# A residual block of a diffusion model on Trainium2: the second normalization's scales handed out one group sooner, with the written order and the engines of the scaled copies planned anew

## The chip, the cores and the metric

The kernel runs on one core of a Trainium2 chip. A core has five engines that work side by side, each through its own list of instructions: PE (TensorE, matrix products; its weight loads are shown apart as PEld), DVE (VectorE), ACT (ScalarE), POOL (GpSimd) and SP (SyncE, which here only starts DMA transfers; POOL starts some too). The metric is the device time of one execution in microseconds (us), lower is better. The profile comes from one execution that was recorded by the hardware profiler.

## The reference

The block takes `x` of shape (2, 512, 64, 64), a time embedding `t_emb` of (2, 1152), two pairs of group norm parameters and three weight tensors, and returns the same shape as `x`. There are 4 groups of 128 channels, so one group of the normalization is exactly one tile of 128 partitions.

```python
def gn(z, gamma, beta):
    zr = z.reshape(B, G, (C // G) * H * W)          # G = 4
    mu = zr.mean(-1).reshape(B, G, 1)
    var = ((zr - mu) ** 2).mean(-1).reshape(B, G, 1)
    zn = ((zr - mu) / jnp.sqrt(var + 1e-5)).reshape(B, C, H, W)
    return zn * gamma.reshape(1, C, 1, 1) + beta.reshape(1, C, 1, 1)

h = conv3(_silu(gn(x, g1, be1)), w1)                # conv3: 3x3, zero padding
h = h + (_silu(t_emb) @ w_emb).reshape(B, C, 1, 1)
h = conv3(_silu(gn(h, g2, be2)), w2)
return x + h
```

## The kernel before, in words

*Layers, chunks, groups.* There are two layers, one for each convolution. A layer is worked off in four chunks (two images, each in two halves of 32 rows), and a chunk in four groups, one for each tile of 128 output channels. So a layer has 16 groups and the kernel 32; "group (1,2)" is group 2 of layer 1. A group keeps PE busy for about 13 us.

*The convolution.* It is not done as nine products but in transformed form: the activations of a chunk are transformed to `V`, the weights to `U`, PE multiplies them, and the products are transformed back. Some products use the untransformed weights `R`.

- `produce_V` makes `V` of one chunk. For each of the four channel tiles, SP loads a piece of the layer's input into `ak` (L621; in layer 1 from the scratch tensor `h_scr` that layer 0 wrote), ACT applies the normalization and SiLU in one instruction (L628, with the scales `sc_all` and biases `nb_all`), and DVE transforms: copies of `ak` by a factor, and L642, L649, L669, L679, L559, L564.
- `prep_U` makes `U` of one output tile and half of the input channels: SP loads `R` and `g1t` (L402), four scaled copies write `U` and `g1t` in place, a POOL DMA that accumulates (L433) and DVE additions (L422) follow, and `nest_U` (L395).
- The matmuls of a group are at L935 (128x512, into the PSUM tiles `acc` and `mid`), at L943 (128x256, into `nst`) and L1038. Evacuations are scaled copies from PSUM: `rm<-nst`, `rm<-mid`, `ring<-acc`. DVE transforms back in L988 to L1009 and others; a POOL DMA adds one part (L1070).
- In layer 0 the result goes to `h_scr` by SP (L1074), and two ACT instructions (L796) for each group take its sum and sum of squares. In layer 1 POOL transfers add `x` (L803) and store the output (L809).

*The second normalization.* When both halves of an image have gone through layer 0, `gn2_me` (L508 to L519, DVE) makes means from the sums of L796 and the embedding. `gn2_scale` (L521 to L527) calls `gn_scale_bias` (L316 to L342): a small PE matmul (L319) sums over partitions and spreads the result, DVE copies and combines (L321, L330, L331, L332), POOL raises the variance to the power -1/2 (L339), DVE multiplies and adds (L340 to L342, L526, L527) and so fills `sc_all` and `nb_all` of layer 1. L628 of that image in layer 1 reads them.

*What sets the order.* The program is written out group by group; a small scheduler (`_Background`) deals out the steps of `produce_V` and `prep_U` to the groups by due times. The function `aux_plan` says at which group `gn2_scale` is emitted: for image 0 in group 11 of layer 0, for image 1 in group 3 of layer 1. But the order in which the engines execute is not that one. After emission, `in_order` takes for each of the five engines a list of numbers, `ORDER` (L64 to L173), and pins the engine's instructions to that order: number k is the k-th instruction that was emitted for this engine. DMA starts on POOL and SP are in these lists as well. When an instruction waits, everything behind it on its engine waits too.

*Which engine copies.* A scaled copy is one instruction with a source, a target and a factor. `scaled_copy` (L302 to L309) can make it on ACT (L308) or DVE (L309), and the string `FLIP` has one bit for each of its 406 calls, in the order of emission: evacuations (`evac`) go to ACT unless their bit is 1, all others (`times`) go to DVE unless it is 1. In the profile, the engine and the tiles tell what such a row is: L308 ACT `rm<-nst` is an evacuation of the nested products, L309 DVE `U<-R` a weight copy.

Of the kernel before, what the change touches and what calls it, by code (L numbers as in the profile page):

```python
# [18 lines left out]
class _Background:  # L19
# [45 lines left out]
0-31 90-122 32-43 123 44-56 124 156 125 157-162 126 163-172 127-136 173-181 137-153 182-187 154-155 57-73 188 74-79  # L65
189-252 80-89 254 286 255 287-317 256-258 253 320-335 259-277 336-351 278-285 318 358 370-385 359-360 352-353
386-401 354-355 319 356-357 364-369 408-410 420-423 402-403 424-435 361-362 414 404-407 415-419 363 411-413 458 461
436-451 459 452-453 460 462-463 454 464-465 455 466 470-485 467 456-457 468-469 486-501 511-512 508 502-503 509
514-519 504-507 510 513 520-525 544-549 526-533 550 534-536 551 537 552-553 538-542 592-593 543 554-559 568 560-565
580 566-567 569-570 581-583 571-572 594 573-575 595 576 584-585 596-600 586-589 601-608 624-625 590-591 626-634 609  # L70
635-638 577-579 639-644 610-621 645 648 622-623 646-647 649-654 673 661 674 655-659 675 660 662-670 689 705-716 671
717-721 672 722-725 676 726-728 677-678 690-701 737 702-703 738 704 679-680 749-750 681-687 751-752 688 753-760
739-744 729-730 745 761 731-736 762 746 763 777 747-748 778-779 793-815 780-786 825-826 787-789 816 827 790-792 837
828 764-776 829-835 838 836 839-848 817 849 865 850-851 818 852 819-822 866-867 853-857 823 868-869 824 870-871 858
872 859 873 860-864 874-879 881 880 882-903 905-907 904 913 908 914-915 925 909 916 926 910-912 937-938 917 927-928
939-940 918 929-931 919 953 941-945 954 920 932 946 921 947-949 922 955-957 950 969 923 951-952 924 958 933-936
959-966 970-974 967-968 975 1001 976-978 1002-1004 1013 979-992 1005 1014-1015 993 1006 1016-1018 994 1025-1026
1019-1022 1027 1023 1028-1030 1007 1024 1031-1032 995-1000 1033-1036 1008-1009 1037-1038 1010-1011 1039-1040 1012
1041 1057-1058 1042 1059-1060 1043 1061 1044-1048 1062-1063 1049-1050 1064-1065 1051-1054 1066-1075 1055-1056
1076-1087 1109 1088 1097 1089 1110-1111 1090-1091 1112-1120 1125-1132 1092-1093 1141 1133 1142 1134-1136 1094 1137  # L80
1095 1138-1140 1098-1099 1121-1124 1100 1096 1101-1108 1143-1147 1157-1172 1148-1156 1173-1181 1185-1193 1182-1183
1194 1184 1195-1209 1213 1210-1212 1214-1242 1245-1260 1243 1261-1262 1285-1291 1263-1264 1244 1265-1267 1301-1302
1268-1284 1303-1315 1317-1319 1292 1316 1320-1327 1293-1295 1328-1332 1296-1300 1349-1353 1361-1362 1354-1357
1333-1348 1363 1358-1359 1373-1381 1360 1364 1382-1386 1365-1367 1387-1389 1405 1390-1394 1368-1371 1395-1404 1372
1406-1429 1437 1430-1431 1438-1441 1432-1436 1442-1443 1450-1451 1444-1448 1452-1459 1462-1463 1460-1461 1464
1478-1493 1449 1494-1495 1465-1477 1496-1502 1526-1528 1538 1529-1531 1539-1541 1510-1518 1542 1503-1509 1543
1519-1525 1532-1537 1544-1551 1566-1581 1552-1565 1582-1614 1626-1627 1615-1619 1628-1631 1638-1639 1620-1624 1632
1625 1633-1636 1654-1661 1637 1662-1670 1640-1653 1671-1701 1726-1730 1702 1731 1703 1732-1737 1704-1705 1714-1716
1706-1710 1717-1719 1711-1713 1720-1725 1742-1744 1738-1741 1745-1746 1758 1747-1749 1759-1760 1750-1757 1761-1770
1774-1777 1790-1798 1778-1785 1799 1802 1814 1771 1786-1787 1772-1773 1800 1803-1804 1788-1789 1805 1815-1816  # L90
1806-1809 1801 1810-1813 1830 1846 1831 1847 1832 1848-1853 1833 1854-1861 1834-1835 1862-1864 1817-1829 1865-1869
1836-1845 1894-1909 1870-1874 1882 1910-1912 1883-1891 1913 1926-1928 1875-1881 1929-1930 1914-1918 1892 1931-1940
1893 1919 1941-1951 1920-1925 1952-1961 1974-1985 1962-1963 1990-1992 1964 1993 1965-1967 2006-2007 1968-1969 2008
1994 2009-2012 1995-2000 1970-1971 2001-2005 2013-2015 1972-1973 2016-2025 2030-2033 2026-2028 2034-2035 1986 2036
2042-2045 2037 2046 2029 2047 1987 2048 1988-1989 2049 2038-2039 2050-2053 2040-2041 2054 2070-2071 2086 2055-2056
2087-2088 2057-2059 2089 2060-2064 2090 2072 2091 2065-2069 2073-2075 2092 2076-2077 2093 2078-2085 2094-2101 2110
2102 2111-2113 2103-2105 2123 2114 2124-2131 2115 2106-2109 2116-2117 2135-2136 2132 2137-2140 2151 2141-2145 2133
2118 2146 2167 2152 2119 2147-2149 2153 2120 2150 2134 2154-2156 2121-2122 2157-2159 2168-2171 2160-2164 2172
2165-2166 2173-2178 2183-2198 2179-2181 2199 2182 2200-2201 2211 2202-2205 2212 2223 2206-2208 2224-2226 2239-2241
2227-2231 2255-2258 2232 2259 2213 2260-2263 2242-2243 2214-2217 2209-2210 2218-2219 2244 2220-2222 2245 2233-2236  # L100
2246 2237-2238 2247-2252 2264 2253-2254 2265-2270 2287-2289 2271-2286 2290-2294 2299-2300 2311-2321 2327 2322
2328-2339 2301 2323-2326 2340-2342 2302-2303 2343-2344 2304 2295 2345 2296-2298 2305-2307 2346 2308-2310 2347-2354
2359-2372 2355-2356 2373 2357-2358 2374 2399-2414 2375-2377 2387-2396 2378-2380 2415-2421 2381-2382 2422-2423
2383-2384 2424-2426 2385-2386 2427-2430 2397-2398 2431-2446 2463-2464 2447-2462 2465-2471 2475 2487 2476 2488-2489
2477-2481 2503-2504 2482-2486 2505 2519-2521 2472-2474 2506-2509 2522-2525 2490-2502 2526 2510-2516 2527-2528
2517-2518 2529-2534 2551-2556 2535-2550 2557-2563 2575-2583 2591 2584 2564-2566 2607 2585-2587 2592 2588-2590 2608
2593 2567 2594 2568-2574 2609-2611 2595-2606 2612-2620 2623-2625 2639 2626-2628 2621-2622 2629 2640-2641 2663
2630-2631 2664-2665 2632-2635 2651 2636-2638 2666-2667 2652 2642 2668 2643-2644 2669 2653-2654 2670 2645-2646
2671-2672 2647-2648 2673-2677 2655 2678-2679 2656-2659 2680 2660 2681 2695 2682 2661 2683-2685 2662 2686-2690
2696-2701 2691-2694 2702-2704 2649-2650 2705-2726 2751-2764 2727-2728 2739 2765-2766 2740 2729-2733 2741-2742  # L110
2734-2737 2743 2767-2769 2744 2738 2770-2772 2783-2784 2773-2777 2745 2778 2746 2779-2780 2747-2748 2785-2786
2781-2782 2749-2750 2787-2798 2815 2799-2807 2816-2820 2808-2812 2821 2813-2814 2827-2828 2822 2829-2836 2823-2825
2837-2838 2826 2839-2840 2855 2841 2856 2871 2842-2846 2872-2875 2857 2847-2849 2876-2878 2850 2858 2851-2853 2859
2854 2860-2861 2879-2882 2862-2870 2883-2885 2887-2901 2886 2902 2935-2939 2903 2911-2913 2940 2904-2905 2941-2943
2914 2944-2950 2915-2917 2951-2953 2906-2908 2954 2909-2910 2955 2967-2968 2956 2969 2957-2962 2918 2970 2963-2966
2919-2926 2971-2972 2927 2973-2975 2928-2934 2976-2980 2983-2985 2981-2982 2986-2996 3031-3032 2999-3000 3033-3034
3001-3003 2997 3035-3036 2998 3037-3039 3007 3004-3005 3008 3006 3040-3046 3009-3011 3047-3048 3063-3064 3015-3022
3065-3070 3012-3013 3071-3074 3014 3075-3078 3049-3062 3079-3088 3023-3030 3089-3094 3159-3160 3095 3171-3173
3096-3097 3174-3175 3161 3176-3177 3162 3111 3127 3112 3128 3113-3116 3098 3117-3120 3099-3110 3129-3130 3121
3131-3133 3122-3126 3134 3143-3158 3135-3142 3178-3180 3183 3181-3182 3163 3184-3189 3164-3166 3207 3167-3169  # L120
3190-3191 3208 3170 3209-3217 3192-3204 3218-3222 3205-3206 3223-3230""",
    "DVE": """
0 4 3 2 1 14 13 5 7 6 48 8 16 9 15 10 17 11 20 12 19 18 25-26 22 27 21 28 23 29 24 30-31 46 32-33 47 49 34 52 35 53
39 36 54 50 37 55 51 38 40 113 115 74 41 56 76 42 57 43 81 58 44 59 45 60 83 61 82 62-64 66 65 67 87 68 88 69-71 84
72 93 92 102 101 103 78 80 85 89 86 114 116 96 73 90 97-100 91 122 94 125 110 134 95 119 104 121 105 117 138 106 135
107 123 108 124 109 136 139 137 120 118 79 126 140 129 141 128 127 111 77 75 142 130 112 145 131 147 164 132 146 133
# [61 lines left out]
def kernel(  # L188
# [622 lines left out]
    def aux_plan(layer, g):  # L811
        acts = []
        if layer == 0:
# [4 lines left out]
            if g == 11:  # L818
                acts.append(lambda k: gn2_scale(k[0], 0))
# [408 lines left out]
```

## Time and profile before

| what | value |
|---|---|
| time, median of 3 runs | 460.15 us (459.83 to 460.62) |
| the profiled execution | 459.56 us, of it the span of the instructions 457.5 us |
| mean granted clock of TensorE | 0.995 |
| HBM read, written | 42.54 MB, 16.78 MB; 130 GB/s over the span |
| matmuls L943 (128x256), L935 (128x512, `acc`), L935 (`mid`) | 1600, 696, 336 |
| copies L308 on ACT `rm<-nst` (128x1024) | 98, mean 1023 ns |
| L628 on ACT (128x2112) | 28, mean 2153 ns |
| POOL's power L339 | 2.02 us for 128x4 |

A profile row such as `192.30 2.02 POOL L339 ... [0.82 <-DVE var L332]` reads: at 192.30 us from the start of the span POOL began an instruction of line 339 that took 2.02 us; it had been idle for 0.82 us, and what ended that idle time was the DVE instruction of line 332 that wrote `var`. A busy share is time in instructions over the span. The digits of a slice are tenths of a fortieth of the span (11.4 us). "Granted clock" is the share of full speed at which TensorE was let run. Matmuls overlap, so the sum of their single durations is more than PE's busy time.

### The profile page before, as it was taken

The page shows a single profiled execution, that of the slowest core. Times are in us where ns is not written, and L with a number is a line of the kernel's source. Part 1 is how long each engine was busy: PE and PEld are TensorE (multiplying, and loading weights), DVE is VectorE, ACT ScalarE, POOL GpSimd, SP SyncE. Part 2 cuts the span into 40 slices and gives each one's busy share as a digit, 9 for nine tenths or more (in the row PEclk, how much of TensorE's full clock was granted, in tenths as well). Part 3 has the DMA queues.
Part 4 walks back from the last instruction along what each step waited for, and adds up shares of the span by engine and source line. Part 5 has one row for each costly group of instructions (what it writes and reads, how often), then busy time and mean ns, then how long its engine had stood idle before and what let it go on. Part 6 is the DMA issues. An engine that isn't in the chain of part 4 may idle for free.

```text
span 457.5 us, 8442 instructions
## 1 busy us (share of the span) xinstructions
PE 444.0 (97%) x3238; PEld 288.3 (63%) x3238; DVE 431.4 (94%) x828; ACT 386.8 (85%) x423; POOL 75.6 (17%) x119
## 2 busy tenths in 40 slices
PE   8989999999999999997999999999999999999996
PEld 7944454556555667665556655557666666668874
DVE  2999999999999999999999999998999989999796
ACT  5899999979998798789999999647878697969761
POOL 1222301020000001210121211113221221222110
PEclk9999999999999999999899999999999999999999
DMA  8999765543846462447879895466957768637654
GB/s 311 353 388 243 153 169 150 161 128 104 192 128 159 101 179 64 122 141 210 221 171 262 219 208 117 115 139 163 214 142 185 181 162 210 138 92 150 128 159 165
DMA packets 25011, 80.05 MB, mean 175 GB/s; under 512 B 2827, under 2 KB 6027, under 8 KB 24587
## 3 DMA queue, kind: packets, MB, share of 16 engines
q0 software_dynamic: 10080, 34.87, 37.4%
q1 hardware_dynamic: 14832, 44.64, 28.8%
q8 instruction: 25, 0.41, 0.3%
q14 instruction: 15, 0.12, 0.1%
q10 hardware_dynamic: 59, 0.01, 0.0%
HBM read 42.54 MB, written 16.78 MB: 130 GB/s over the span
## 4 chain that ended last, share of the span: by engine, by line
PE 66%; DVE 18%; ACT 6%; issue 5%; DMA 2%; POOL 1%; SPq 0%; DVEq 0%; ACTq 0%; POOLq 0%
PE nst L943 26%; PE acc L935 23%; PE mid L935 13%; DVE V L679 2%; DVE ak L642 2%; DMA xbuf<-in_x_dram 2%; PE acc L1038 2%; DVE V L559 1%; ACT ak L628 1%; ACT rm L308 1%; ACT ring L796 1%; PE half L935 1%; DVE ak L649 1%; DVE V L564 1%; DVE V L669 1%
## 5 line engine op out<-in xcount | busy, mean ns | idle before, releaser
L943 PE MATMUL nst<-V,U 128*128 128x256 f16 x1600 | 209.5, 272 | 3.6 <-DVE rm L309 2.4
L943 PEld LDWEIGHTS <-U 128*128 128x128 f16 x1600 | 153.8, 97 | 54.8 <-issue 4.7
L935 PE MATMUL acc<-V,R 128*128 128x512 f16 x696 | 182.7, 385 | 2.0 <-DVE V L669 0.9
L935 PEld LDWEIGHTS <-R 128*128 128x128 bf16 x744 | 71.7, 97 | 64.9 <-issue 3.3
L308 ACT ACTIVATE rm<-nst 128x1024 f16<-128x1024 f32 x98 | 97.7, 1023 | 10.2 <-PE nst L943 4.7
L935 PE MATMUL mid<-V,U 128*128 128x512 f16 x336 | 85.1, 384 | 0.7 <-DVE U L422 0.7
L796 ACT ACTIVATE ring<-ring 128x2048 f16<-128x2048 f16 x32 | 61.3, 1914 | 1.6 <-ACT ak L628 0.6
L628 ACT ACTIVATE ak<-ak,nb_all,sc_all 128x2112 f16<-128x2112 f16 (+1 forms) x28 | 60.1, 2153 | 2.3 <-DVE nb_all L527 2.3
L935 PEld LDWEIGHTS <-U 128*128 128x128 f16 x336 | 32.4, 97 | 36.1 <-DVE U L422 1.4
L308 ACT ACTIVATE ring<-ring 128x512 f16<-128x512 f16 x58 | 34.9, 626 | 22.7 <-DVE ring L1002 15.9
L1070 POOL DMA_DIRECT2D ring<-ring x28 | 26.5, 946 | 143.3 <-ACT ring L308 122.1
L308 ACT ACTIVATE ak<-ak 128x520 f16<-128x520 f16 (+1 forms) x34 | 38.2, 1141 | 3.0 <-DVE ak L649 2.8
L642 DVE TENSOR_TENSOR ak<-ak 128x2080 f16<-128x2080 f16 x32 | 39.9, 1248 | 0.1
L679 DVE TENSOR_TENSOR V<-ak 128x1040 f16<-128x1040 f16 x54 | 39.2, 726 | 0.7 <-ACT ak L308 0.5
L990 DVE TENSOR_TENSOR rm<-tu,rm 128x1024 f16<-128x1024 f16 x50 | 34.8, 695 | 1.0 <-ACT rm L308 0.8
L564 DVE TENSOR_TENSOR V<-V 128x512 f16<-128x512 f16 (+1 forms) x62 | 35.3, 577 | 0.0
L559 DVE TENSOR_TENSOR V<-V 128x1024 f16<-128x1024 f16 (+1 forms) x31 | 30.8, 995 | 0.7 <-PE acc L935 0.7
L308 ACT ACTIVATE ring<-acc 128x512 f16<-128x512 f32 x52 | 29.6, 596 | 1.8 <-DVE ring L309 0.8
L422 DVE TENSOR_TENSOR U<-U,g1t 128x1536 f16<-128x1536 f16 x32 | 30.9, 972 | 0.0
L989 DVE TENSOR_TENSOR tu<-rm 128x512 f16<-128x512 f16 x50 | 21.4, 428 | 2.7 <-ACT rm L308 2.5
L649 DVE TENSOR_TENSOR ak<-ak 128x1040 f16<-128x1040 f16 x32 | 23.0, 718 | 0.1
L669 DVE TENSOR_TENSOR V<-ak 128x1040 f16<-128x1040 f16 x32 | 22.9, 715 | 0.0
(132 smaller groups left out, 452.4 us busy)
## 6 DMA issues: line engine op xcount, KB each, us to landing
ring<-ring POOLq DMA_DIRECT2D x28, 512.0 KB, 4.6
ak<-h_scr SPq DMA_DIRECT2D x16, 528.0 KB, 3.9
h_scr<-ring SPq DMA_DIRECT2D x16, 512.0 KB, 3.7
ring<-in_x_dram POOLq DMA_DIRECT2D x14, 512.0 KB, 5.6
out_dram<-ring POOLq DMA_DIRECT2D x14, 512.0 KB, 4.7
ak<-in_x_dram SPq DMA_DIRECT2D x12, 528.0 KB, 4.3
R<-in_w_dram SPq DMA_DIRECT2D x16, 384.0 KB, 4.7
U<-U POOLq DMA_DIRECT2D x14, 384.0 KB, 5.7
```

Source lines behind the costliest of these rows:

```text
L308: return nc.scalar.activation(out=o, in_=i, func=ACT.Copy, scale=f)
L422: nc.vector.tensor_tensor(out=o, in0=i0, in1=i1, op=op)
L559: nc.vector.tensor_tensor(out=lo2.rearrange("p c q (t w) -> p (q t) c w", w=HALF), in0=plane_pair(0, HALF + 2), in1=plane_pair(1, HALF), o ...
L564: nc.vector.tensor_tensor(out=hi2[:, c].rearrange("p q (t w) -> p (q t) w", w=HALF), in0=i0, in1=i1, op=op)
L628: nc.scalar.activation(out=at[:, lo - r0:hi - r0, 1:W + 1], in_=sap, func=ACT.Silu, bias=nb_all[:, layer, b, ct:ct + 1], scale=sc_all[:, l ...
L642: nc.vector.tensor_tensor(out=diff, in0=diff, in1=below, op=ALU.add)
L649: nc.vector.tensor_tensor(out=rows(1, 2), in0=rows(1, 2), in1=rows(3, 2), op=ALU.subtract)
L679: nc.vector.tensor_tensor(out=o, in0=in0, in1=in1, op=op)
L796: behind(nc.scalar.activation(out=junk, in_=y, func=func, scale=scale, accum_out=acc), inst)
L935: nc.tensor.matmul(out, lhsT=w_direct(pos, ct, kx), rhs=rhs, start=first, stop=last)
L943: nc.tensor.matmul(accs["nst", (pos - 1) // 2][bank][:, q, :, plane, :], lhsT=lhsT, rhs=rhs.rearrange("p (t w) -> p t w", w=HALF), start=s ...
L990: nc.vector.tensor_tensor(out=msl[:, 1 - k:4 - k:2].rearrange("p q t w -> p q (t w)"), in0=tu[:].rearrange("p q t e w -> p q (t e w)"), in ...
```

## The change

Three things change, and no instruction of the computation is added or dropped.

1. For image 0, `gn2_me` is emitted in group 9 of layer 0 and `gn2_scale` in group 10, each one group sooner; for image 1, `gn2_scale` is emitted in group 2 of layer 1 rather than 3, while its `gn2_me` stays at group 1. So 28 instructions of the two chains stand earlier in the emission.
2. All five lists in `ORDER` are written anew.
3. `FLIP` has other bits, 406 as before. DVE has 3 instructions fewer (824 to 821 in the program) and ACT 3 more (385 to 388). By form: `U<-R` 128x768 on DVE 24 to 19 and on ACT 8 to 13, `U<-R` 128x1536 on DVE 7 to 9 and on ACT 9 to 7, `ak<-ak` 128x2080 on DVE 19 to 18 and on ACT 13 to 14, `g1t` on DVE 8 to 9 and on ACT 8 to 7, `ring<-ring` on DVE 26 to 28 and on ACT 58 to 56, `ring<-acc` on DVE 4 to 3 and on ACT 52 to 53, `qs` on DVE 1 to 0 and on ACT 11 to 12.

The lists are long; of each only a piece is shown.

```diff
 ORDER = {
     "PE": """
-0-31 90-122 32-43 123 44-56 124 156 125 157-162 126 163-172 127-136 173-181 137-153 182-187 154-155 57-73 188 74-79
+0-26 90-105 27-30 106-122 31-47 123 48-60 124 156-158 125-155 159-187 61-67 188 68-81 189-252 82-89 254 286-288 253
...
     "DVE": """
-0 4 3 2 1 14 13 5 7 6 48 8 16 9 15 10 17 11 20 12 19 18 25-26 22 27 21 28 23 29 24 30-31 46 32-33 47 49 34 52 35 53
...
     "Activation": """
...
     "Pool": """
-0 4 1 10 5 11 2-3 6-7 12-13 8-9 21 14 22 15-17 19 18 20 24 23 25 28 27 30 29 26 32-33 31 37 34 39 35 40 36 42 38 41
+0 4 1 10 5 11 2-3 6-7 12 8 13 9 21 14-16 22 17-20 24-25 23 28 27 26 30 32 29 33 31 37 39 34-35 40 42 36 38 41 47
...
     "SP": """
-0-13 17 19 21 18 23 20 14 25 15-16 22 28 30 33 24 26 29 27 31 35 32 37 34 36 42 39 38 40 44 43 41 45 48 46 49 47 50
+0-13 17 19 21 18 23 25 20 14-16 28 22 30 33 24 26 29 31 27 35 32 37 34 36 42 39 38 40 44 43 48 41 45 50 46 49 47 54
...
-    FLIP = "0100100011000000000000100010010100000110100001110111001100001100110000000011000000010011100000111001...
+    FLIP = "0110100011000000000000100010010100010010100001110111011100001000110100000101000000010011000001011100...
...
-            if g == 11:
+            if g == 10:
                 acts.append(lambda k: gn2_scale(k[0], 0))
         else:
-            if g == 3:
+            if g == 2:
                 acts.append(lambda k: gn2_scale(k[0], 1))
         return acts
...
-                if (layer, grp) in ((0, 10), (1, 1)):
+                if (layer, grp) in ((0, 9), (1, 1)):
                     gn2_me(layer, st2[layer])
```

More of the change, by code (lines that the diff above doesn't have):

```diff
@@ L70 @@
[L70 to L74, printed above, removed]
@@ new lines @@
+3210-3230""",
+    "DVE": """
+0 2-4 1 13 5 7 6 47 8-10 14-16 11 25 12 18-19 24 17 26 21 27 20 28 22-23 29 31-32 30 45 33 46 34 48 35 51 49 73 52
+38 50 36 53 37 55 54 75 39 56 40 114 112 72 57 80 86 41 58 42 82 59 43 81 44 62 108 91 60 87 61 88 63 83 64 101 65
+92 66 77 79 67 69 68 100 70 113 84 71 85 89 115 90 121 124 93 109 94-99 133 102 118 103 134 104 120 137 105 135 106
+136 78 107 119 143 123 122 116-117 138 76 74 128 139 144 127 125 110 126 129 111 140 130 163 145 131 141 132 142
+151-152 146 153 147 170-172 164 154 173 155 184 149 148 156 165 150 185 157 166 158 186 159 174 160 175 161 176 162
@@ L163 @@
+299 297-298 300-303 310 306 305 304 311 309 307-308 315 313 316 314 312 322 317-318 323 319-320 327-328 321 325-326
+324 332-333 329-330 334-335 339 336-337 340 338 331 342 341 346-347 343 350-351 344-345 348-349 353 352 362 361 358
+357 354 363-364 356 355 359-360 366 365 370-371 367 369 374 368 373 375 372 377 376 378 380-381 379 382 384 383 385
+387 386""",
     "Pool": """
[L164 to L165 removed]
+0 4 1 10 5 11 2-3 6-7 12 8 13 9 21 14-16 22 17-20 24-25 23 28 27 26 30 32 29 33 31 37 39 34-35 40 42 36 38 41 47
@@ L171 @@
+51 68 71 56 52 73 57 53 59 55 61 58 63 60 65 62 67 70 66 72 64 86 75-76 78 77 80 69 81 87 74 82 84 83 88 79 85
+89-102""",
 }
```

178 lines of the change are left out of this document (85 added, 93 removed).

## The prediction

> **What bounds the kernel now.** I read first the page's shares and slices, then a table of busy time by stretch, then the waits of TensorE, then the timeline around the second normalization. The shares and slices:
>
> ```profile
> PE 444.0 (97%) x3238; PEld 288.3 (63%) x3238; DVE 431.4 (94%) x828; ACT 386.8 (85%) x423; POOL 75.6 (17%) x119
> PE   8989999999999999997999999999999999999996
> DVE  2999999999999999999999999998999989999796
> ACT  5899999979998798789999999647878697969761
> ```
>
> PE is the bound on average and DVE is close behind it; PE's one weak inner slice is the nineteenth, 206 to 217 us, where layer 0 goes over into layer 1. By stretch (us, then busy time of PE, PEld, DVE, ACT, POOL with instructions, granted clock, DMA share, GB/s):
>
> ```profile
> 8.00:48.00 40.00, 36.63 (x472) 24.07 (x470) 38.05 (x101) 35.92 (x32) 9.26 (x12) 1.00 0.98 328
> 48.00:196.00 148.00, 148.00 (x933) 87.32 (x932) 145.39 (x275) 132.35 (x145) 18.48 (x27) 1.00 0.52 137
> 196.00:235.00 39.00, 34.97 (x250) 24.41 (x248) 38.94 (x76) 37.69 (x40) 5.00 (x9) 0.96 0.68 190
> 235.00:290.00 55.00, 55.00 (x325) 31.19 (x323) 54.70 (x104) 53.95 (x58) 10.20 (x14) 1.00 0.86 200
> 290.00:320.00 30.00, 30.00 (x200) 19.06 (x198) 28.43 (x58) 17.30 (x22) 6.83 (x8) 1.00 0.54 132
> ...
> 217.50:221.00 3.50, 3.50 (x15) 1.87 (x14) 3.50 (x8) 3.26 (x5) 1.73 (x2) 0.51 0.62 164
> ```
>
> The reader is to see that only 196 to 235 us leaves PE idle after the start, that DVE (38.94 of 39) and ACT (37.69 of 39) are both full there, and that the clock was halved for 3.5 us. The waits inside it, and the chain that makes the scales (start us, duration, engine; in brackets the idle time before and its releaser):
>
> ```profile
> 192.30 2.02 POOL L339 TENSOR_TENSOR var<-var,neg_half 128x4 f32<-128x4 f32 x1 [0.82 <-DVE var L332]
> 194.35 0.16 DVE L340 TENSOR_TENSOR sc_all<-var,gb 128x4 f32<-128x4 f32 x1 [0.93 <-POOL var L339]
> 196.18 2.15 ACT L628 ACTIVATE ak<-ak,nb_all,sc_all 128x2112 f16<-128x2112 f16 x1 [2.32 <-DVE nb_all L527]
> 215.47 1.23 DVE L309 TENSOR_SCALAR rm<-nst 128x1024 f16<-128x1024 f32 x1
> 216.75 2.85 PE L943 MATMUL nst<-V,U 128*128 128x256 f16 x16 [2.37 <-DVE rm L309]
> ```
>
> PE loses 6.2 us here: 1.0 at 201 (acc, for its evacuation on DVE), 2.5 at 214.2 to 216.75 (nst, for the DVE copy of 1.23 us), 1.7 by the halved clock behind that gap (3.41 us at half speed), 1.0 at 232 (nst, for an ACT copy). Three small waits at 326 to 360 lose 0.95. Elsewhere from 48 us on, matmuls start every 222 ns (L935) and 109 ns (L943).
>
> **The change, part by part.** The times are summed against the profiled execution, 459.56 us (span 457.5 and 2.1 around it), which is 0.59 below the median of 460.15. Nearly every instruction is the same; what differs is their order, and the engine of some copies. To price an order I added up, in the old and the new list of each engine, the durations of the rows that stand ahead of an instruction: "work ahead".
>
> *The scales sooner.* Of image 0, the small matmul L319 stands 10 us earlier. In the new list 21 DVE instructions stand between L332 and L340, where 2 stood, so POOL's 2.02 us is covered and the 0.93 us of DVE idle goes. If those 21 were late themselves the 0.93 would stay; it is the low end, 0.93 the high one. But nb_all (L527) has 0.15 us more DVE work ahead of it: it lands when it did, and the first L628 of layer 1 starts no sooner. The second L628 now stands directly behind it (7 us less ACT work ahead), the fourth 3.3 less. Image 1 is the same: its matmul comes 9.8 us sooner, 8 instructions cover POOL, nb_all keeps its place, and ACT's idle there (1.43 us at 315) is not where PE waits. POOL's and SP's queues: L339 starts sooner on POOL between transfers of 0.9 us each, and the layer-1 weight transfers (L433) issue up to 7 us later; the tightest in the trace is issued at 281.6 and first read at 295.5, takes 5.7 to land and so keeps about 1 us. I cost that at nothing; with the cover gone it would be a wait of up to 1 us.
>
> *The engines of the copies.* DVE has 3 fewer, ACT 3 more, and sizes are swapped: by the row means (DVE 128x768 367 ns, 128x1536 565, 128x2080 705, 128x512 303; ACT 852, 1487, 1943, 626) DVE loses 1.3 us of work and ACT gains 2.3. Most lies in layer 1's group (1,1), about 235 to 290 us: DVE -0.8, ACT +1.7, where ACT has 1.05 us of idle in 55.
>
> *The junction.* The 201-us wait is released by work ahead: its matmul has 2.5 us more PE work ahead. The 216.75 wait has 0.67 us more PE work ahead and its copy, still on DVE, the same DVE work, so alone it shrinks from 2.5 to 1.9. The 232 wait's ACT copy has 0.86 us less work ahead. But DVE and ACT are gapless, so the sum of the waits, not each of them, is set by what they have ahead. With PE at 222 and 109 ns, the new DVE list makes PE lose at least 3.25 us up to 256 (4.2 if the 0.93 stays); the new ACT list 4.4 up to 226 (3 if ACT's idle of 2.3 before L628 is filled). Before, they took 6.2. Last comes ACT in group (1,2), 294 us: a mid matmul (L935) waits for a copy with 2.24 us more work ahead, and had 0.66 us to spare, so PE gains there between 0 (the idle before L628 stays) and 2.5 (it is filled). This is the tightest bound and sets the end. Between 0 and 2.5 I take 1.2: the second L628 behind the first fills that idle only in part, since nb_all lands no sooner.
>
> *The start and layer 0.* In 24 to 48 us the new DVE order delays PE by 1.2 us; between 88 and 106 PE would wait up to 2.7 us longer, for V (L679) and ring copies (L308) that now have 1.4 to 6.4 us more work ahead. Ends: 0, and 1.2 and 2.7. I take 0, since PE then only arrives later at 196, where DVE and ACT make it wait anyway: the same loss, put earlier. That holds only while the gap there does not halve the clock. *The rest:* 0.95 at 326 to 360 is unchanged (between -0.95 and +0.95); one copy in (1,14) goes from DVE (0.30) to ACT (0.63), up to +0.33 at the end, taken as 0 since ACT is idle there (1.86 busy of 11).
>
> Sum: 459.56 - 1.2 = 458.36, plus 0.59 gives 458.95, so 458.9.
>
> On the halved clock: here a gap of 2.5 us was enough, with the clock at 0.51 from 217.5 to 221. The Trainium skill (TensorE: Matmul & The Clock Gate, Why this matters for your kernels) asks for no TensorE gaps above about 3 us, and puts the fall at one window of idle. By that rule no gap here would have cost, and the junction would be worth 4.5, not 6.2. The trace disagrees by 0.5 us of gap, so I count by the trace: 2.5 halves, 1.0 doesn't.
>
> **The rivals.**
> - *Faster by more.* ACT's 2.3 us idle is filled, no gap reaches 2 us, the clock stays whole: the full 2.5 of room is used, 457.65; with the three small waits gone too, 456.7. For it: the second L628 is ready 7 us sooner. Against: L527 lands no sooner.
> - *Nothing changes.* The gap at 216.75 stays near 2.5, the clock halves again, and DVE and ACT are the late ones as before: losses 5.5 to 6.2, 459.5 to 460.15. For it: the copy of 1.23 us stays on DVE with the same work ahead. By the skill's rule, which needs 3 us, this case would end 1.7 lower; no run here shows it.
> - *Slower: ACT becomes the bound.* If L628 starts at 196.2 and the idle before it stays, the copy in group (1,2) is late by 2.24 - 0.66 = 1.6 us: 461.7. It decides once ACT's list up to 292 us is more than 0.66 us later than before. For it: ACT was busy 53.95 of 55 and gains 1.7 there. Against: 12.7 us of ACT idle follow in 290 to 320, so it is paid once.
> - *Slower: layer 0.* The waits at 88 to 106 fall together into one gap above 2.5 us and halve the clock: 2.7 + 1.7 - 1.2 = 3.2, 463.3, unless DVE makes PE wait at 196 anyway.
>
> **How the numbers follow.** The forecast 0.32 (own range 458.0 to 459.8); faster by more 0.16; nothing 0.19; ACT bound 0.25; layer 0 0.08. 0.2% is 0.9 us, about what a measurement can tell from no change: below 459.2 counts as faster. Faster: 0.16 and 0.27 of the forecast's, 0.43. Same: 0.05 of the forecast's, 0.16 of nothing, 0.21. Slower: 0.25, 0.08 and 0.03 of an unforeseen wait beside nothing, 0.36. Range: down to 456.7, where the small waits go too; up to 462.4, the ACT case with a halved clock's remainder of 0.7; the layer-0 case and half of the lowest are left out, about 1 in 8.
>
> **What would show it.** In the changed profile: the idle before L340 gone and L527 at 195 to 196; the idle before the first L628 of layer 1 below 1.5 us; no gap above 2 us between 196 and 235 and the clock above 0.96 there; waits of PE of 1 to 3 us in all at 88 to 106 with the clock whole; 294 us without a PE wait on an ACT copy above 1 us. Wrong if the clock is halved in layer 0, if a weight transfer is read late, or if ACT's copy at 294 is the longest PE wait.

## The result, and the profile after

The changed kernel takes 458.58 us (median of 6 executions, 457.94 to 458.94), the kernel before 459.99 in the same comparison: a ratio of 0.9972, with a 95% interval from 0.9962 to 0.9983, or 1.3 us less. The forecast was 458.9. The profiled execution took 458.73 us (before 459.56), so it shows 0.83 of it. In the profile after, line numbers are 2 lower (L943 is L941). Shares and slices first:

```profile
PE 443.9 (97%) x3238; PEld 287.8 (63%) x3238; DVE 430.0 (94%) x825; ACT 387.9 (85%) x426; POOL 78.3 (17%) x119
PE   7998999999999999999989999999999999999996
PEclk9998999999999999999999999999999999999999
```

The weak slice at 206 to 217 us is full now. The first slice is a tenth lower, the dent of the third (23 to 34 us) has moved to the fourth (34 to 46 us), where the granted clock falls too, and a new one stands in the twenty-first (228 to 240 us). The stretches, in the columns used before:

```profile
8.00:48.00 40.00, 35.98 (x461) 23.54 (x459) 36.99 (x96) 35.55 (x34) 8.80 (x12) 0.96 0.98 325
48.00:196.00 148.00, 147.60 (x928) 86.89 (x927) 146.29 (x282) 132.26 (x140) 21.71 (x27) 1.00 0.52 140
196.00:235.00 39.00, 36.89 (x265) 25.29 (x263) 37.94 (x74) 37.93 (x40) 6.10 (x11) 1.00 0.71 185
235.00:290.00 55.00, 54.80 (x326) 31.28 (x324) 54.97 (x100) 54.36 (x64) 9.02 (x13) 1.00 0.81 194
...
36.00:39.50 3.50, 3.01 (x23) 1.33 (x23) 3.50 (x7) 3.50 (x5) 1.29 (x2) 0.52 1.06 217
```

Between 196 and 235 us PE gained 1.9 us of busy time and the clock is whole; from 8 to 48 us it lost 0.65, and the clock was halved at 36. The scales, the two gaps ahead of the halved clock, and the longest wait of the junction:

```profile
187.60 2.25 POOL L337 TENSOR_TENSOR var<-var,neg_half 128x4 f32<-128x4 f32 x1 [6.00 <-DVE var L330]
193.10 0.16 DVE L338 TENSOR_TENSOR sc_all<-var,gb 128x4 f32<-128x4 f32 x1
195.83 0.16 DVE L525 TENSOR_TENSOR nb_all<-nb_all,t 128x4 f32<-128x4 f32 x1
...
33.77 1.27 PE L933 MATMUL acc<-V,R 128*128 128x512 f16 x5 [0.79 <-DVE V L667]
36.49 0.58 PE L933 MATMUL mid<-V,U 128*128 128x512 f16 x1 [1.08 <-DVE V L677]
231.22 2.46 PE L941 MATMUL nst<-V,U 128*128 128x256 f16 x21 [1.39 <-ACT rm L306]
```

POOL's power is over long before L338 asks for it; nb_all lands at 195.83 + 0.16 = 195.99, where it landed at 195.94 + 0.16 = 196.10 before.

Where the time went shows when both are compared at the same amount of PE work. For each matmul I took the median start-to-start time of its kind (222 ns, 109 ns and so on) as its work and added up; "lag" is how much later than the kernel before an execution had done so much. Rows are profiled executions of this kernel and of those in the experiments:

| kernel | lag at 45 us of work | at 190 | at 260 | at 360 | at 440 |
|---|---|---|---|---|---|
| (time of the kernel before) | 53.5 | 198.4 | 274.7 | 375.6 | 453.2 |
| changed | +2.5 | +2.9 | +0.1 | -0.85 | -0.8 |
| changed, second profile | +1.9 | +2.6 | -0.6 | -1.5 | -0.1 |
| start_before | +0.9 | +2.6 | +0.1 | -0.8 | +0.2 |
| layer0_before | +0.4 | +1.5 | +0.4 | -0.5 | +0.3 |
| switch_305 | +3.5 | +3.9 | +1.0 | +1.0 | +1.0 |
| act_light | +1.4 | +2.2 | -0.2 | -1.1 | -0.9 |
| dve_light | +1.4 | +2.3 | -0.4 | -1.3 | -1.3 |
| rm_sooner | +2.5 | +3.0 | +1.0 | +0.1 | +0.1 |
| pool_covered | +0.2 | +0.1 | -1.3 | -1.0 | -1.0 |
| late_alone | +0.3 | +0.2 | -0.3 | -1.2 | +0.2 |
| mix_282 | +0.3 | +0.2 | -0.5 | -1.5 | +0.2 |
| order_alone | +1.7 | +3.9 | +2.4 | +2.1 | +3.8 |
| load_behind_store | +2.5 | +3.2 | +1.1 | +0.2 | +0.2 |

In the changed kernel PE loses 2.9 us up to the end of layer 0, wins it back at the junction (190 to 260 us of work), and gains 0.9 where the three small waits of before were (260 to 360). Between 360 and 440 some executions lose 0.8 to 1.7 us in one place. The experiments take these four in turn. Each row is one execution, and rows of the same order differ: load_behind_store has the changed kernel's order up to 379 us and leaves the junction 1.0 us later than the first profile of the changed kernel, 1.7 later than the second.

### The profile page after: what moved, and what is told of

It is laid out like the page before. It is cut to its first block, busy times and chain, and to the rows that moved or that the text cites. A ratio compares the mean times of both kernels' runs of the same rounds, so it can differ in the third digit from the quotient of the medians.

```text
span 456.7 us, 8448 instructions
## 1 busy us (share of the span) xinstructions
PE 443.9 (97%) x3238; PEld 287.8 (63%) x3238; DVE 430.0 (94%) x825; ACT 387.9 (85%) x426; POOL 78.3 (17%) x119
## 4 chain that ended last, share of the span: by engine, by line
PE 46%; DVE 7%; DMA 4%; ACT 4%; issue 3%; DVEq 0%; POOL 0%; POOLq 0%; ACTq 0%
PE nst L941 23%; PE acc L933 17%; PE mid L933 3%; DMA ring<-ring 3%; PE acc L1036 2%; DMA h_scr<-ring 1%; PE half L933 1%; ACT rm L306 1%; ACT ring L794 1%; DVE rm L988 1%; ACT ring L306 1%; DVE V L677 1%; DVE ring L1000 1%; DVE V L562 1%; ACT ak L626 0%
## 5 line engine op out<-in xcount | busy, mean ns | idle before, releaser
L941 PE MATMUL nst<-V,U 128*128 128x256 f16 x1600 | 204.3, 271 | 1.9 <-ACT rm L306 1.7
L941 PEld LDWEIGHTS <-U 128*128 128x128 f16 x1600 | 153.8, 96 | 48.1 <-issue 2.7
L933 PE MATMUL acc<-V,R 128*128 128x512 f16 x696 | 177.4, 384 | 1.4 <-DVE V L667 1.1
L933 PE MATMUL mid<-V,U 128*128 128x512 f16 x336 | 86.8, 387 | 2.0 <-DVE V L677 1.5
L794 ACT ACTIVATE ring<-ring 128x2048 f16<-128x2048 f16 x32 | 61.1, 1908 | 3.6 <-DMA ring<-ring 3.0
L306 ACT ACTIVATE ring<-ring 128x512 f16<-128x512 f16 x56 | 33.7, 624 | 22.0 <-DVE ring L1000 14.2
L1068 POOL DMA_DIRECT2D ring<-ring x28 | 24.4, 871 | 137.4 <-ACT ring L306 120.7
L306 ACT ACTIVATE ak<-ak 128x520 f16<-128x520 f16 (+1 forms) x35 | 40.4, 1166 | 3.7 <-DVE ak L647 3.5
L677 DVE TENSOR_TENSOR V<-ak 128x1040 f16<-128x1040 f16 x54 | 38.1, 707 | 0.7 <-ACT ak L306 0.5
L562 DVE TENSOR_TENSOR V<-V 128x512 f16<-128x512 f16 (+1 forms) x62 | 33.6, 557 | 0.0
L306 ACT ACTIVATE U<-R 128x768 f16<-128x768 bf16 (+1 forms) x20 | 20.9, 1065 | 1.8 <-DMA R<-in_w_dram 1.8
```

The costliest lines, as they stand in the source:

```text
L306: return nc.scalar.activation(out=o, in_=i, func=ACT.Copy, scale=f)
L562: nc.vector.tensor_tensor(out=hi2[:, c].rearrange("p q (t w) -> p (q t) w", w=HALF), in0=i0, in1=i1, op=op)
L677: nc.vector.tensor_tensor(out=o, in0=in0, in1=in1, op=op)
L794: behind(nc.scalar.activation(out=junk, in_=y, func=func, scale=scale, accum_out=acc), inst)
L933: nc.tensor.matmul(out, lhsT=w_direct(pos, ct, kx), rhs=rhs, start=first, stop=last)
L941: nc.tensor.matmul(accs["nst", (pos - 1) // 2][bank][:, q, :, plane, :], lhsT=lhsT, rhs=rhs.rearrange("p (t w) -> p t w", w=HALF), start=s ...
```

## The experiments

Each is compared with the kernel before on its own chip. Most kernels here are built from the two written lists: an engine runs the one list up to a moment, and what is left in the order of the other. Of such lists only the first changed line is shown.

**Is the loss ahead of the junction paid?** start_before takes the start from before:

```diff
     "PE": """
-0-26 90-105 27-30 106-122 31-47 123 48-60 124 156-158 125-155 159-187 61-67 188 68-81 189-252 82-89 254 286-288 253
+0-31 90-122 32-43 123 44-56 124 156 125 157-162 126 163-172 127-136 173-181 137-153 182-187 154-155 57-73 188 74-79
...
```

> The changed kernel, but with the order and the copy engines of the kernel before for what that kernel began in its first 47.5 us; computes all of the reference. In the profiles the change put TensorE 2.5 us further behind by 50 us, yet at 264 us both kernels stood at the same point of TensorE's work. Theory A (DVE and ACT set when the junction of the layers ends, so a loss of TensorE ahead of it is free): TensorE arrives 2.5 us sooner at 190 us, waits 2.5 us more between 196 and 262 us, and the time stays that of the change, 458.6, from 458.2 to 459.0. Theory B (TensorE's loss in the start is paid): 458.6 - 2.5 = 456.1.

Measured: 458.78 us against 459.51, ratio 0.9984 (0.9972 to 0.9995). Nothing like the 2.5 us is gained. The granted clock was 0.998 or more in all 12 executions, so the halved clock of the start is gone with its gaps, and even that does not show at the end. But the run tells less than was expected of it. By the table PE was 0.9 us late at 45 us of work and lost another 1.7 in layer 0, so it came to the junction only 0.3 us sooner than the changed kernel, not 2.5: the loss spared in the start comes back before the junction, and theory A is not tested by this run.

layer0_before takes all of layer 0 from before; its first changed line is the same, and so are the bits of `FLIP` up to there.

> The changed kernel, but with the order and the copy engines of the kernel before for all that it began up to 176 us (start and nearly all of layer 0); computes all of the reference. TensorE should then stand at 168.06 us after 160 us of its work, 3.05 us sooner than with the change. Theory A (DVE and ACT set the end of the junction): 458.6 all the same, 458.0 to 459.2. Theory B (the loss is paid): 458.6 - 3.05 = 455.5. If only the waits at 326 to 360 us count, this and A agree.

Measured: 459.55 against 459.51, ratio 0.9998 (0.9983 to 1.0012). PE reaches the junction at 199.9 us, 1.4 sooner than the changed kernel (201.4), and leaves it at 275.1, 0.4 later: it waited 2.17 us for one ACT copy at 204. So in this profile the 1.4 us by which PE came sooner are lost again at the junction, as theory A has it. The time missed A's range (458.0 to 459.2) on the slow side all the same; by the ratios it is 1.2 us slower than the changed kernel. The profile shows 0.4 of that at the junction and a loss of 0.8 at 388, which neither theory had; that the order of layer 0 gives ACT and DVE a lead there is a guess that no run here shows.

**Where is the gain made?** switch_305 goes back to the old order at 305 us:

```diff
     "DVE": """
...
-580 570 556 581 557 582 574 583 575 584 576 585-586 577 560 587 578 561 589 592 588 593 573 562 594 590 610 591
+553 529 554 559 548-549 555 571 550 572 569 579 568 558 580 570 556 581 557 582 574 583 575 584 576-577 586 585 578 560
...
```

> The changed kernel up to what it began at 305 us, and from there on the order and the copy engines of the kernel before; computes all of the reference. In the profiles all of the gain, 0.83 us, comes after 300 us, where three waits of TensorE (0.41, 0.33 and 0.21 us at 326, 351 and 359 us) are gone. Theory A (the gain is these waits, and they come of the order there): the waits come back, 458.6 + 0.9 = 459.5. Theory B (the gain is made at the junction and before, in ACT's and DVE's lead): the waits stay away, 458.6.

Measured: 459.48 against 459.51, ratio 1.0001 (0.9990 to 1.0013): by the median the gain is gone. The median hides two groups: the five executions with a clock of 0.995 or less took 459.7 to 461.0, and the seven at 0.998 or more have a median of 458.9, which is 0.65 below the kernel before. So the time alone does not settle it; the profiles do. First two of the three waits in the kernel before, then two in switch_305 (the bracket counts from the modelled end of the last matmul; from start to start PE loses 0.41 and 0.33, then 0.33 and 0.31 us):

```profile
326.43 1.92 PE L943 MATMUL nst<-V,U 128*128 128x256 f16 x16 [0.24 <-ACT rm L308]
351.19 1.92 PE L943 MATMUL nst<-V,U 128*128 128x256 f16 x16 [0.17 <-ACT rm L308]
...
313.90 2.24 PE L938 MATMUL nst<-V,U 128*128 128x256 f16 x19 [0.17 <-ACT rm L303]
352.18 1.92 PE L938 MATMUL nst<-V,U 128*128 128x256 f16 x16 [0.15 <-ACT rm L303]
```

A third of 0.21 stands at 359 and at 360. The changed kernel's first profile has no such wait from 262 us to the end. The lag of switch_305 stays at +1.0 from 260 on, where the changed kernel gains 0.9. So in the profiles theory A holds: the waits come with the old order, two of them at their old places and the first at 314 instead of 326. That profile also came 3.9 us late to the junction, behind some 7 us of halved clock in the start, and left it 1.0 late; how much the junction can hide is not one number, as is shown below.

late_alone is the mirror: the old order up to 282 us, the new one behind it.

```diff
     "PE": """
...
-1994 2009-2012 1995-2000 1970-1971 2001-2005 2013-2015 1972-1973 2016-2025 2030-2033 2026-2028 2034-2035 1986 2036
+1994 2009-2012 1995-2000 1986 2001-2003 1970 2004 1971-1973 2013-2014 2005 1987-1988 2015 1989 2016-2017 2031-2033
...
-            if g == 3:
+            if g == 2:
```

> The kernel before for all that it began up to 282 us, and the order and copy engines of the change from there (with image 1's scales emitted a group sooner); computes all of the reference. Theory A (the gain of the change is the three waits of 0.95 us at 326 to 360, which its order there takes away; the junction nets nothing): 459.5 - 0.85 = 458.7, ratio 0.998 or a little below. Theory B (the late order helps only behind the changed junction): 459.5, ratio 1.000.

Measured: 460.12 against 459.92, ratio 1.0002 (0.9989 to 1.0016). By its profile theory A is right up to 360 us of work (lag -1.2, the three waits gone), and then 1.4 us are lost at 388. Of the two it is the better evidence that the gain of 0.9 is made by the order behind 282 us. In the time at the end it missed; in the profiled execution the loss at 388, which the expectation lacked, took the gain back.

**The scales alone.** pool_covered is the kernel before with L330 to L332 moved up on DVE (numbers 366 to 368, which stood apart and now follow 365; the list is wrapped anew, so the two lines do not begin at the same number):

```diff
-351-352 358 365 362 366 363 367 359 368 364 360 369 361 370 372 375 371 374 373 356 376-380 382 381 387 383 398 388
+337 336 333 338-339 354 340 355 345-346 341 347 342 348 344 349 357 350 343 351-352 358 365-368 362-363 359 364 360 369
```

> The kernel before, with one edit: the three DVE instructions L330 to L332 of image 0 stand directly behind L321, so that POOL's power of 2.02 us starts about 1.5 us sooner and DVE has work while it runs; computes all of the reference. The idle of 0.93 us ahead of L340 should go. If DVE's list sets the junction, up to 0.9 of it is gained: 460.0 - 0.9 = 459.1. If ACT or the halved clock sets it, nothing: 460.0, from 459.7 to 460.3. The prediction had counted it as a part of its gain of 1.2.

Measured: 458.75 against 459.51, ratio 0.9989 (0.9978 to 1.0000), about 0.5 us. The idle of 0.93 is gone, and L628 (L625 there) starts at 195.63, not 196.18. The surprise is behind it: the gap at 216 is the same, but the clock stays whole.

```profile
216.18 1.92 PE L940 MATMUL nst<-V,U 128*128 128x256 f16 x16 [2.36 <-DVE rm L306]
...
217.50:221.00 3.50, 3.50 (x21) 1.83 (x19) 3.50 (x7) 3.50 (x5) 1.73 (x2) 1.00 0.65 144
```

What differs is where the gap lies. The traces record when the granted clock changes, and in all of them the changes lie whole multiples of 3.413 us apart; in the kernel before they are at 5.92, 217.55, 220.96 and 456.48 us. On this grid the gap of 2.5 us falls into one stretch in the kernel before, 214.13 to 217.55, in which PE is busy for 1.05 us, and the clock is halved in the next stretch. In late_alone (1.05 us) and mix_282 (1.06) it is the same. In pool_covered the grid cuts the gap in two, PE is busy for 2.96 us in the one stretch and 1.51 in the next, and the clock stays whole. Busy time is not all of the rule: 1.89 us in the start of the changed kernel (32.74 to 36.15) was followed by half a clock, 1.51 here was not. mix_282 has pool_covered's order up to 282 us and the halved clock; at 260 us of work it is 0.5 ahead of the kernel before, and pool_covered 1.3. So by these two profiles 0.8 of pool_covered's 1.3 goes with the whole clock, and 0.5 with the covered power.

**Which engine holds the junction?** after_again is the changed kernel once more:

> The changed kernel itself, to have it on the same chip as the three kernels below; computes all of the reference. Its ratio to the kernel before was 0.9972 (0.9962 to 0.9983). Expected 0.9972 again, 1.3 us below the kernel before, with executions of lower granted clock (0.995, half clock at 36 to 40 us in the start) 0.5 us above those at 0.999.

Measured: 458.69 against 459.54, ratio 0.9974 (0.9958 to 0.9989). The executions at 0.991 to 0.992 of the clock took 459.1, 459.2 and 461.1; the others split into six at 457.3 to 458.4 and three at 459.0 to 459.5.

rm_sooner reorders the longest wait of the junction:

```diff
-419 416 420 417 446 421 448 418 447 414 413 422 428-429 423 461 424 430 436 432 468 467 427 431 434 453 433 454 435
+419 416 420 417 446 421 448 418 447 414 413 422 428-429 423 461 424 430 432 431 436 468 467 427 434 453 433 454 435
...
-146-147 149-150 153 163 151 154-157 152 159 158 160 164 161-162 168 165-167 189 175 171 169-170 172 188 173 191 174
-179-180 177-178 229 182 181 201-202 176 185-187 192-193 183 194-195 203 184 197-198 196 199 204-205 200 230 206 209
+146-147 149-150 153 163 151 154-157 152 159 158 160 164 161-162 168 165-167 189 175 171 169-170 172 188 173 179-180
+191 174 177-178 229 182 181 201-202 176 185-187 192-193 183 194-195 203 184 197-198 196 199 204-205 200 230 206 209
```

> The changed kernel with one local edit at its longest inner wait (TensorE waits 1.55 us at 231.2 for the copy rm<-nst on ACT): the two DVE instructions that read the old rm stand ahead of a copy and two weight copies on DVE, and the two rm copies ahead of a weight copy of 1.49 us on ACT; computes all of the reference. Theory O (the wait is a matter of order): it goes, and about 1.5 us stays gained, 457.1. Theory S (ACT's and DVE's whole work up to 262 us sets when the junction ends): the wait comes back between 235 and 262 us as ACT's and DVE's work is the same, and the time stays 458.6, from 458.2 to 459.0.

Measured: 460.18 against 459.54, ratio 1.0012 (0.9999 to 1.0026), some 1.5 us slower than the changed kernel. The wait at 231 fell from 1.55 to 0.30 us, two came in its place, and one of 0.31 at 253 grew to 0.82:

```profile
233.29 5.47 PE L933 MATMUL acc<-V,R 128*128 128x512 f16 x24 [0.97 <-ACT ring L306]
246.41 1.92 PE L941 MATMUL nst<-V,U 128*128 128x256 f16 x16 [0.28 <-ACT rm L306]
253.72 2.60 PE L933 MATMUL mid<-V,U 128*128 128x512 f16 x11 [0.66 <-ACT rm L306]
```

What was put back on ACT, a weight copy and a `ring` copy with the evacuations behind them, was itself awaited. So the local wait is not a matter of its own order alone, and the time is above the range that theory S gave.

Two kernels take work away, one from ACT and one from DVE. act_light:

```diff
+            n_sums[0] += 1
+            if n_sums[0] > 12:
+                y, junk = y[:, 0:y.shape[1] // 2], junk[:, 0:junk.shape[1] // 2]
```

> The changed kernel, but the sums and sums of squares (L796) of the last four groups of layer 0 run over half of their columns, so the second normalization of image 1 is computed from fewer values; this leaves out 8 x 0.9 = 7.2 us of ACT work between 208 and 255 us. If ACT sets the end of the junction, most of the waits of TensorE there (2.9 us ended by ACT between 196 and 262) go: 458.6 - 2.5 = 456.1. If DVE sets it: 458.6, down to 458.2.

Measured: 458.88 against 459.54, ratio 0.9993 (0.9978 to 1.0009), no faster than the changed kernel (0.9974), with 7 us less for ACT. Its profile shows who was waiting (L1004 is L1000 of the changed kernel):

```profile
228.74 0.69 DVE L1004 TENSOR_TENSOR ring<-rm 128x1024 f16<-128x1024 f16 x1
...
229.47 0.63 ACT L306 ACTIVATE ring<-ring 128x512 f16<-128x512 f16 x1 [1.89 <-DVE ring L1004]
230.01 1.92 ACT L306 ACTIVATE rm<-nst 128x1024 f16<-128x1024 f32 x2
231.06 2.46 PE L945 MATMUL nst<-V,U 128*128 128x256 f16 x21 [1.39 <-ACT rm L306]
```

ACT now stands idle for 1.89 us, and PE's wait, put down to ACT, is as long as before (1.55 from start to start). The cause is one step further: DVE's L1004 reads the only `rm` tile and fills `ring`, and DVE has no idle ahead of it.

And dve_light:

```diff
-                nc.vector.tensor_tensor(out=diff, in0=diff, in1=below, op=ALU.add)
+                e = CR * WP // 2 if layer == 1 and b == 0 else CR * WP
+                nc.vector.tensor_tensor(out=diff[:, 0:e], in0=diff[:, 0:e], in1=below[:, 0:e], op=ALU.add)
```

> The changed kernel, but the subtraction of rows on DVE (L642) runs over half of its columns for the four channel tiles of the first two chunks of layer 1, which leaves part of V of image 0 wrong; this takes 8 x 0.6 = 4.8 us of DVE work away between 200 and 290 us, half of it before 232. If DVE sets the end of the junction: up to 2.4 us gained, 456.2. If ACT sets it: 458.6, down to 458.2.

Measured: 457.46 against 459.54, ratio 0.9950 (0.9934 to 0.9966), 1.2 us below the changed kernel's. But at the junction its profile is only 0.4 us ahead of the changed kernel's, and 0.2 behind the second one's. There L1001 ends 0.4 us before ACT, busy with a weight copy, gets to the `ring` copy behind it: with DVE lighter, ACT is last at once. So DVE holds that wait, and ACT stands about half a microsecond behind it. The gain was expected to be made at the junction, and missed there. None of its five executions is near 459, so it may lie in the place at 388 that is taken up below; five executions cannot show that.

Two things ahead of the junction move it from one execution to the next, and no expectation had them. The first is a transfer. In the changed order ACT waits at 185 us for a sum (L796, here L794) until POOL's accumulating transfer of `ring` (L1070) has landed, first the kernel before, then the changed one:

```profile
181.72 1.91 ACT L796 ACTIVATE ring<-ring 128x2048 f16<-128x2048 f16 x1 [0.36 <-DMA ring<-ring]
...
185.16 1.91 ACT L794 ACTIVATE ring<-ring 128x2048 f16<-128x2048 f16 x1 [1.95 <-DMA ring<-ring]
```

In five profiles (changed twice, act_light, dve_light, load_behind_store) nb_all lands 10.83 us after this instruction starts, at 195.47 to 196.81. The latest is load_behind_store: it waited 2.76 us for the transfer, came 3.2 us late to the junction and left it 1.1 late, with the order of the changed kernel, which came 2.9 late and left it 0.1 late.

The second is POOL's power. In start_before, layer0_before, switch_305 and rm_sooner it took 5.98 us, where it took 2.02 to 2.28 elsewhere, and DVE again stood idle for 0.93 us ahead of its next step (L340 before, L338 in the change), although 10 instructions stand in between as in the changed kernel. Why it takes that long in some executions is open. The lags of these four at 260 (+0.1 to +1.0) contain this idle, so they are no clean measure of what their edits do at the junction.

**What are the engines of the copies worth?** order_alone is the changed order with the old engines:

```diff
     "DVE": """
-0 2-4 1 13 5 7 6 47 8-10 14-16 11 25 12 18-19 24 17 26 21 27 20 28 22-23 29 31-32 30 45 33 46 34 48 35 51 49 73 52
+0 2-4 1 13 5 7 14 6 48 8-10 15-17 11 26 12 19-20 25 18 27 22 28 21 29 23-24 30 32-33 31 46 34 47 35 49 36 52 50 74 53
...
```

> The changed kernel with the copy engines of the kernel before (35 copies go back to where they were, each put into the other list by the time at which it ran in the change); computes all of the reference. DVE gets 1.2 us more work, 0.8 of it in 235 to 290 us, and ACT 1.8 less. If DVE sets the end of the junction: 458.7 + 1.0 = 459.7. If ACT does: 458.7 - 1.0 = 457.7. The prediction had ACT as the tightest bound there, so its working gives the second.

Measured: 462.16 against 459.92, ratio 1.0055 (1.0036 to 1.0073): by the ratios 3.7 us slower than the changed kernel. That is the sign of the DVE theory and over three times its size. The profile has a wait of 1.2 us at 167, where the change has none, and one of 1.0 at 219, where it has 0.3; it leaves the junction 2.4 late and loses 1.65 at 388. Part of it may be that a copy put into the other list by its old time is not where a planner would put it; how much was not tried.

**The place at 388.** mix_282 joins pool_covered and late_alone (its lists differ from the kernel before in the lines shown for these two).

> The kernel before with L330 to L332 directly behind L321 (POOL's power covered), up to what it began at 282 us, and the order and copy engines of the change from there; computes all of the reference. If the two gains are independent: 458.75 (POOL covered alone) - 0.85 = 457.9, ratio 0.997, better than both kernels by 0.1 to 0.7. If TensorE, arriving 1.3 us sooner behind the junction, only waits for DVE again at 320 to 360: 458.7.

Measured: 460.24 against 459.92, ratio 1.0008 (0.9992 to 1.0024). At 360 us of work the profile is 1.5 us ahead, 0.5 of it made up to 260 and 0.9 behind, so the two gains do add; at 388 it loses 1.7. The second profile of the changed kernel has the same loss, and shows what it is:

```profile
378.89 0.56 POOL L807 DMA_DIRECT2D out_dram<-ring  x1 [2.63 <-DMA ring<-in_x_dram]
379.15 0.32 SPq L619 DMA_DIRECT2D ak<-h_scr  x1
...
385.02 0.69 DVE L1000 TENSOR_TENSOR ring<-rm 128x1024 f16<-128x1024 f16 x1 [1.59 <-DMA out_dram<-ring]
...
387.86 2.13 PE L941 MATMUL nst<-V,U 128*128 128x256 f16 x18 [1.23 <-ACT rm L306]
```

An output store (L809 before) is issued by POOL and a load of `ak` (L621) by SP within half a microsecond; DVE waits for the store to free its ring buffer. Over the profiled executions:

| load issued behind store, us | store lands after, us | PE's wait at 388, us | kernels |
|---|---|---|---|
| 0.12 to 0.36 | 5.5 to 6.3 | 0.8 to 1.7 | changed (second), start_before, layer0_before, late_alone, mix_282, order_alone |
| 0.41 to 0.58 | 4.4 to 5.0 | none | before, changed (first), switch_305, pool_covered, rm_sooner, act_light, dve_light |

The packets of the two DMA queues bear this out; POOL's transfers go through the software queue, SP's through the hardware queue. In the 2.7 us behind the store's issue the changed kernel's first profile has 198 packets of the software queue and none of the other, its second 104 and 23, and mix_282 69 and 60. So where the load is issued early, its packets run between those of the store, or ahead of them.

load_behind_store makes the load wait for the store:

```diff
-                nc.sync.dma_start(
+                ld = nc.sync.dma_start(
...
+                if (layer, b, ch, ct) == (1, B - 1, NCH - 1, CT - 1):
+                    after(ld, stores[7])
...
-            behind(nc.gpsimd.dma_start(out=dst, in_=y), zi)
+            stores.append(behind(nc.gpsimd.dma_start(out=dst, in_=y), zi))
```

> The changed kernel with one more wait: the last load of ak from h_scr (issued at 379 to 381 us) waits until the output store issued just ahead of it has landed; computes all of the reference. In the profiles so far a wait of TensorE of 0.8 to 1.7 us at 388 stands in just those executions where the load was issued 0.12 to 0.36 us behind the store, and in none where it was 0.42 to 0.58 behind; the wait's chain is store late, DVE L1000 idle, rm<-nst on ACT, nst on TensorE. Theory R (store and load share the transfer engines, and the order in which they are issued decides): the wait is never there, the executions of 459.0 to 459.5 go down to 457.3 to 458.4, median 457.9, ratio 0.996. Theory N (the store's landing varies for another reason): 458.7 as the change, with the wait in some executions; if the load itself then lands too late for L626, slower than that.

Measured: 458.30 against 459.71, ratio 0.9963 (0.9947 to 0.9978). In its profile the load is issued at 384.64, the store lands 4.2 us after its issue, and DVE's step runs on time:

```profile
380.27 0.56 POOL L810 DMA_DIRECT2D out_dram<-ring  x1 [2.33 <-DMA ring<-in_x_dram]
...
385.01 0.68 DVE L1003 TENSOR_TENSOR ring<-rm 128x1024 f16<-128x1024 f16 x1
```

Nine of its 12 executions lie between 457.4 and 458.9, three at 459.4 to 459.9 (two of these with a clock of 0.991 and 0.995); the profiled one is the slowest, 459.91, and left the junction 1.1 late. The profile bears theory R out; the time agrees with it, but its interval overlaps that of the changed kernel. By the ratio it is the fastest version that computes all of the reference, 1.7 us below the kernel before; by the medians it is 1.4, no more than the changed kernel had, so a gain on that kernel is not shown.

## Why the prediction was right, and where it was not

- *The time* came out at 458.58 where 458.9 was forecast, inside the likeliest case's own range, and with the right sign. But the sum reached it by two wrong terms that made up for each other: the 1.2 us were to be gained at the junction, where the first profile gains nothing against the kernel before, and the three small waits were to stay, where 0.9 is gained. That the size came out was luck.
- *The scales.* In the changed kernel it came as forecast: the idle ahead of L340 went, nb_all lands when it did, the idle of 2.32 us ahead of the first L628 was partly filled (0.82 is left, ahead of two copies). Covering POOL in the kernel before gave about 0.5, between the two ends named. The reasons hold less well. In the profile 10 DVE instructions stand between L332 and L340, not 21, and in four other profiles they did not cover POOL's power. nb_all lands when it did because a transfer of `ring` landed when it did, not by DVE's work ahead alone. The transfer at 281.6 us that was named as the tightest of the weights is L803's load of `x`; the last of the weights (L433) starts at 269.35. No addition of the weights (L422) waited for a transfer in the changed kernel, as forecast.
- *The junction, taken at 1.2 us gained.* Wrong in size: from 190 to 260 us of work PE lost 6.2 us before and 3.4 after, which is 2.9 better and nearly the lowest bound from DVE's list (3.25); but it came there 2.9 us late, so at 260 us of work the lag is +0.1 in the first profile and -0.6 in the second. With load_behind_store, +1.1, three profiles of this order span 1.7 us there.
- *ACT in group (1,2) as the tightest bound.* This step failed. The copy ended 1.3 us later than before (293.58 against 292.27), not 2.24, which fits with part of ACT's idle being filled, and the mid matmul at 294.23 waited for nothing. DVE held the junction's longest wait, as act_light shows; the rival that ACT becomes the bound did not come.
- *The start and layer 0, taken at 0.* Borne out by one profile: in layer0_before PE came to the junction 1.4 us sooner and left it no sooner (start_before does not test it). Mis-sized in itself: 2.5 us and a halved clock in the start rather than 1.2, and 0.56 rather than up to 2.7 in layer 0. The halved clock at 36 us is one of the signs that the prediction had named for being wrong; it did not decide the time.
- *The three waits of 0.95, taken as unchanged.* Wrong, and this is the term that makes the gain of the first profile: 0.9 of it went, goes as well when only the order behind 282 us is new (late_alone), and does not go with the old order there (switch_305). The upper end of the gain had been named, at 0.95.
- *"2.5 halves, 1.0 doesn't."* Wrong. By the profiles it also counts how a gap lies in the grid of 3.413 us: pool_covered has the same gap of 2.5 us and a whole clock; the changed kernel's clock halved at 36 us behind gaps of 0.8 and 1.1 us, and in its second profile it did not. Of the 1.7 us counted for it at the junction little was paid at the end either: over 61 executions of the kernel before with a clock of 0.9965 or less the mean is 459.90 us, over 38 at 0.9985 or more 459.66. Where in each of them the clock fell is not on record. The Trainium skill (TensorE: Matmul & The Clock Gate, What's actually happening) states that the window in which activity is judged is free-running and does not start with the kernel; the runs agree, in that one and the same order is halved in some executions and not in others.

## What to carry to other kernels

Where another engine's list ends a stage, price a change by what it does to that list and to the waits behind the stage, and expect PE's own losses ahead of it to be free in part, since they take the place of waits: here 2.8 of 2.9 us in one profile and 2.1 of 3.2 in another. The engine that a wait is put down to is the last link: take work from it and see whether it falls idle (1.89 us here) before calling it the cause. And look at pairs of transfers issued within half a microsecond of each other on two queues: whose packets go first may be worth as much as the change.

## What had not been expected

A load issued 0.12 to 0.36 us behind a store goes with a landing of the store after 5.5 to 6.3 us and a wait of PE of 0.8 to 1.7 us; issued 0.41 to 0.58 us behind it, with 4.4 to 5.0 us and no wait. The changed kernel's own two profiles lie on the two sides. The wait took back the whole gain in the profiles of late_alone and mix_282, both ahead by 1.2 to 1.5 us until there. What makes the interval fall on one side or the other in a given execution was not settled; it was 0.49 and 0.26 in the two profiles of the changed kernel. Nor was it expected that the same power of POOL would take 2.0 to 2.3 us in some profiles and 5.98 in others.
